# Ordering loads of v against transposed strips in the opening of a gated attention and mixer kernel

## The chip, the cores and the metric

The kernel runs on one core of one Trainium2 chip. The metric is the device time of one execution in microseconds (us), the median of several runs; less is better. A core has a matrix engine (TensorE, PE in the profile), three engines for elementwise work (VectorE, DVE; ScalarE, ACT; GpSimd, POOL) and a queue engine (SyncE, SP). Each works through its own list of instructions in order. Transfers run on 16 DMA engines, which are fed by two queues here: a software queue, whose transfers GpSimd issues, and a hardware queue, whose transfers SP issues.

## What is computed

```python
def _attn_ref(u, v, z):
    B, S, D = u.shape                                  # 8, 3136, 256; z has 64 columns
    scores = (1.0 / S) * np.matmul(z, z.transpose(0, 2, 1))
    attn = np.maximum(scores, 0.0) ** 2
    out = np.matmul(attn, v)
    return (u * out).astype(np.float32)

def _moe_ref(x, U, V, w_ch1, w_ch2):                   # x is the result of _attn_ref
    h = x.transpose(0, 2, 1) @ U @ V
    u = x + h.transpose(0, 2, 1)
    return (u + np.maximum(u @ w_ch1, 0.0) @ w_ch2).astype(np.float32)
```

The scores of a batch are a symmetric matrix of 3136 x 3136, and the same z stands on both sides. The change concerns the attention part alone.

## The kernel before

**Tiles.** The sequence of a batch is cut into NT = 25 blocks of 128 rows (the last, number NF = 24, has 64). The output block o is the sum over all blocks j of attn[j, o] times v[j]. As the score matrix is symmetric, only half of it is computed: tile `A[j]` holds the block row j against the NB = 13 blocks j to j + 12 (counted around the end). The other blocks that output o needs are transposes of blocks of `A[o]`. A DMA transpose on SP's queue writes them to a `strip`, 12 blocks of 128 x 128 in bf16 (`turn`, line 392). `block` (line 466) picks the tile: from `A[j]` when (o - j) mod 25 is at most 12, else from the strip of o.

**Order of outputs.** Outputs are taken from block 12 on (FIRST = 12): place i in the order is block 12 + i. LEAD = 16 is thus output 4 by place and LEAD + NG = 20 output 8 by place. Where the text below says output 16 to 24, blocks are meant. Two outputs form a pair that shares an accumulator; the first of a pair also takes the half row of block 24 for its partner (lines 551 to 554), so it ends with a read of the partner's strip.

**A score.** `score` (line 352) is a TensorE product of z with itself into PSUM, a ReLU on ScalarE (line 372) and a square on VectorE (line 374). A strip can go only when all of its `A` tile is squared.

**The opening.** `start_up` (line 768) does outputs 12 to 19 of batch 0 by hand, because nothing has been computed yet. For outputs 12 to 15 it makes the needed blocks directly. Meanwhile it scores `A[16]` to `A[19]` and turns each to a strip as soon as it is done (`turned`, line 437). Then outputs 16 to 19 are summed, first from `A`, then in `tail` (line 885) from the strips of 16, 17, 18 and 19 in this order; the steps of the list `rest` beside them make the blocks of `A[15]` to `A[8]` that output 20 needs. `turn(0, 20)` stands before `tail` in the program (line 884), and the strips of 21 and 22 are turned inside it. From place 8 on (output 20), the loop at line 957 runs `attend_steps` (line 526) for each output with the scores of later tiles spread between them.

**Loads of v.** The v of a batch comes in nine pieces (`V_PARTS`, line 311): eight of three blocks each, 192 KB in SBUF, cast to bf16 by the DMA, and the tail. All are issued by GpSimd, as are the loads of u (`load_u`, line 452) and of the weights. Batch 1's v isn't read until batch 0's outputs are done. Pieces 0, 1 and 2 are issued in the opening behind the weights (line 798). Pieces 3 and 4 stand behind a one-column GpSimd copy into the tile `mark`, which reads the strip of output 19 (line 869) and so holds GpSimd until that strip has landed. The tail piece and pieces 5 to 7 come later, out of the loop.

**Output 20.** For it alone the order of blocks is changed (line 530): five from `A` (20 down to 16), then the strip, then eight from `A` (15 down to 8).

**Queues.** SP's list holds only the transposes here, in program order: a strip that waits keeps the strips behind it from being issued. GpSimd's list holds its copies and loads, likewise in order.

Of the kernel before, what the change touches and what calls it, by code (L numbers as in the profile page):

```python
# [42 lines left out]
def kernel(  # L43
# [11 lines left out]
    nc = tc.nc  # L55

    B, S, D = u.shape
# [13 lines left out]
    NB = HALF + 1  # L71
    FIRST = HALF
    AHEAD = 4
    LEAD = FIRST + AHEAD
    NG = 4
# [20 lines left out]
    mark = persist.tile([P, 1], BF16, name="mark")  # L96
# [29 lines left out]
    v_both = [persist.tile([P, NT, D], BF16, name=f"v{k}") for k in range(2)]  # L126
# [5 lines left out]
    def turns(i):  # L132
        return (FIRST + i) % NT
# [168 lines left out]
    def load_v(b, part):  # L302
        t0, t1 = part
        v_bf = v_both[b % 2]
        if t0 < NF:
            pool_dma(out=v_bf[:, t0:t1, :], in_=rows(v[b])[:, t0:t1, :])  # L306
        else:
            for r in halves:
                pool_dma(out=v_bf[r, NF, :], in_=v[b, NF * P :, :])

    V_PARTS = [(t, t + 3) for t in range(0, NF, 3)] + [(NF, NT)]
# [36 lines left out]


    strips = {}  # L350

    def score(b, parts):

        ps = pair_psum()
        zT = zT_of(b)
        zT_flat = zT.rearrange("p t c -> p (t c)")
        at = (min(b, 1), 0)
        for k, (j, c, n, _) in enumerate(parts):
            mm(  # L359
                out=ps[:, k, :n],  # L360
                lhsT=zT[halves[k], j + at[k], :],
                rhs=zT_flat[halves[k], c + at[k] * P : c + at[k] * P + n],
                start=True,
                stop=True,
            )
        if parts[0][3] is parts[-1][3]:
            n = parts[0][2]
            todo = [(parts[0][3], ps[:, :, :n] if len(parts) == 2 else ps[:, 0, :n])]
        else:
            todo = [(part[3], ps[:, k, : part[2]]) for k, part in enumerate(parts)]  # L370
        for dst, src in todo:
            nc.scalar.activation(out=dst, in_=src, func=AF.Relu, scale=sc)  # L372
        for dst, _ in todo:
            nc.vector.tensor_tensor(out=dst, in0=dst, in1=dst, op=ALU.mult)  # L374
# [16 lines left out]

    def turn(b, o):
        strip = strip_pool.tile([P, HALF, P], BF16, name="strip")
        transpose(out=strip, in_=A[o][:, P:])
        strips[b, o] = strip

# [40 lines left out]
    def turned(b, j):  # L437
        steps = score_steps(b, j)
        s = steps.pop()
        return steps + [lambda: (s(), turn(b, j))]  # L440
# [5 lines left out]
    def pair_of(o):  # L446
        first = 0 if o < FIRST else FIRST
        stop = FIRST if o < FIRST else NT
        t0 = o - (o - first) % 2
        return t0, min(2, stop - t0)  # L450

    def load_u(b, o):
        t0, n = pair_of(o)
        u_sb = u_pool.tile([P, 2, D], FP32, name="u_sb")
        if o < NF:
            pool_dma(out=u_sb[:, :n, :], in_=rows(u[b])[:, t0 : t0 + n, :])  # L456
        else:
            for r in halves:
                pool_dma(out=u_sb[r, 0, :], in_=u[b, NF * P :, :])
        u_tiles[b, t0] = u_sb  # L460

    def open_pair(b, o):
        acc[pair_of(o)[0]] = sets[opened[0] % 2]
        opened[0] += 1

    def block(b, o, j):
        k = (o - j) % NT
        return A[j][:, k * P : (k + 1) * P] if k <= HALF else strips[b, o][:, NT - 1 - k, :]

    def half(b, o, j, h, w, start, stop, **kw):  # L470
        t0, _ = pair_of(o)
        mm(  # L472
            out=acc[t0][h][:, (o - t0) * D : (o - t0 + 1) * D],
            lhsT=w[halves[h]],
            rhs=v_both[b % 2][halves[h], j, :],
            start=start,
            stop=stop,
            **kw,
        )

    def close_pair(b, o):
        t0, n = pair_of(o)
        banks, u_sb = acc.pop(t0), u_tiles.pop((b, t0))
        w = n * D
        both = both_pool.tile([P, 512], FP32, name="both")
        nc.scalar.copy(out=both[:, :w], in_=banks[1][:, :w])  # L486
        nc.vector.tensor_tensor(  # L487
            out=both[:, :w], in0=banks[0][:, :w], in1=both[:, :w], op=ALU.add
        )
        if o == NF and b == 0:  # L490

            for bank in banks:
                for r in range(2):
                    q = both[halves[r], :w]
                    nc.vector.tensor_tensor(out=q, in0=bank[halves[1 - r], :w], in1=q, op=ALU.add)
        elif o == NF:
            for r in range(2):
                nc.scalar.copy(out=both[halves[r], w : 2 * w], in_=both[halves[1 - r], :w])
            nc.vector.tensor_tensor(
                out=both[:, :w], in0=both[:, :w], in1=both[:, w : 2 * w], op=ALU.add  # L500
            )
        nc.vector.tensor_tensor(  # L502
            out=x_at(b, t0, n),
            in0=split(both[:, :w]),
            in1=u_sb[:, :n, :].rearrange("p t (a c) -> p t a c", c=P),
            op=ALU.mult,
        )

    def quarter(b, j, n, h):

        c = n % 2
        mm(  # L512
            out=acc[NF][h][halves[c], :D],
            lhsT=block(b, NF, j)[halves[h], halves[c]],
            rhs=v_both[b % 2][halves[h], j, :],
            start=(n < 2),
            stop=(n == (NT - 2 if c else NT - 1 - 2 * h)),
        )

    def after(b, o):  # L520

        t0, n = pair_of(o)
        i = place(t0) + n
        return (b, turns(i)) if i < NT else (b + 1, turns(0))

    def attend_steps(b, o):
        t0, n = pair_of(o)
        last = t0 + n - 1
        js = [(o - k) % NT if k < NB else (o + k - HALF) % NT for k in range(NT)]
        if b == 0 and o == LEAD + NG:  # L530
            js = js[: NG + 1] + js[NB:] + js[NG + 1 : NB]
        js.remove(NF)

        def step(i):
            if i == 0 and o == t0:
                open_pair(b, o)
            if i == 16 and o == t0 and after(b, o)[0] < B:
                load_u(*after(b, o))
            if o == NF:
                if i < NT - 1 and i % 2:  # L540
                    for n in (i - 1, i):
                        for h in range(2):
                            quarter(b, js[n], n, h)
                elif i == NT - 1:
                    quarter(b, NF, i, 0)
            elif i < NT - 1:
                w = block(b, o, js[i])
                end = i == NT - 2
                half(b, o, js[i], 0, w, i == 0, end and o > t0)
                half(b, o, js[i], 1, w, i == 0 and o == t0, end)  # L550
            elif o == t0:
                half(b, o, NF, 0, block(b, o, NF), False, True)
                if o < last:
                    half(b, o + 1, NF, 1, block(b, o + 1, NF), True, False)
            if i == NT - 1 and o == last:
                close_pair(b, o)

        return [lambda i=i: step(i) for i in range(NT)]
# [209 lines left out]
    def start_up():  # L768
# [4 lines left out]
            out=eye,  # L773
            in_=eye,
# [20 lines left out]
            load_z(1, WHOLE)  # L795
        run(fetches)
        if B > 1:
            for part in V_PARTS[:3]:
                load_v(1, part)
        nxt = [s for j in range(LEAD, LEAD + NG) for s in turned(0, j)]  # L800
        rooms = [A[j % NT][:, : 2 * NG * P] for j in range(LEAD + NG, LEAD + 3 * NG)]
# [64 lines left out]
        ]  # L866
        run(_merge(nxt[2:], own))
        if B > 1:
            nc.gpsimd.tensor_copy(out=mark, in_=strips[0, LEAD + NG - 1][:, 0, :1])
            for part in V_PARTS[3:5]:  # L870
                load_v(1, part)
        rest = [
            lambda pair=pair: make_stored(pair, LEAD + NG)
# [3 lines left out]
        for i, pair in enumerate(pairs):  # L877
            if i + 2 < len(pairs):
                make_stored(pairs[i + 2], LEAD)
            else:  # L880
                more.pop(0)()
            use_stored(pair, outs)
            if i == len(pairs) - 1:
                turn(0, LEAD + NG)
        tail = []
        for o in outs:
            js = [(o + 1 + i) % NT for i in range(HALF)]
# [49 lines left out]

    fetches, second_w, puts, copies = weight_steps()
    panel = start_up()
    puts = dict(zip((17, 18, 19, 20, 16, 21, NT), puts + copies))  # L940
    late = []
# [6 lines left out]
    for b in range(B):  # L948
# [8 lines left out]
        for i in range(begin, NT):  # L957
            o = turns(i)
# [7 lines left out]
            if more:  # L966
# [14 lines left out]
                if b == 0 and i == 15:  # L981
                    mirror_z((0, FIRST))
                    extend_z(b + 1)
            main = attend_steps(b, o)
            if b and i in ahead:
                at = 17 if (i + (i > FIRST)) % 2 == 0 else 12 if i == 7 else 9 if i == 3 else 10
# [39 lines left out]
    b = B - 1  # L1026
# [46 lines left out]
```

## Time and profile before

| what | us |
|---|---|
| median of 3 runs (lowest to highest) | 995.57 (993.81 to 998.08) |
| profiled execution | 995.98 |
| span of the profiled execution | 994.3 |
| TensorE busy | 978.9 (98%) |
| TensorE weight loads busy | 815.5 (82%) |
| ScalarE busy | 615.5 (62%) |
| VectorE busy | 552.7 (56%) |
| GpSimd busy | 169.5 (17%) |
| hardware queue (transposes, last stores) | 371520 packets, 96.14 MB |
| software queue (loads, stores) | 28320 packets, 66.28 MB |

The span is what the profiler saw between the first and the last instruction; the execution's own time is 1.7 us longer. TensorE works at its full granted clock throughout (1.00). A row of a timeline gives start and duration in us, engine, line and operation, the tiles written and read, how many instructions were merged into it (x16), and in brackets the idle time of the engine before it with what ended it. "Landing" is the time from the issue of a transfer to its completion. Rows for stretches of time give, for TensorE, weight loads, VectorE, ScalarE and GpSimd in this order, the busy us and the number of instructions, then the granted clock, the mean busy share of the DMA engines and the GB/s that they moved.

Strips of the opening, from SP's queue:

| strip of output | issued at | landing after | landed |
|---|---|---|---|
| 16 | 20.22 | 11.0 | 31.2 |
| 17 | 26.60 | 8.4 | 35.0 |
| 18 | 30.51 | 7.0 | 37.5 |
| 19 | 33.05 | 5.6 | 38.7 |
| 20 | 37.07 | 3.8 | 40.9 |
| 21 | 38.95 | 8.7 | 47.7 |
| 22 | 40.92 | 13.7 | 54.6 |
| 23 | 47.16 | 9.9 | 57.1 |

Pieces of batch 1's v: issued at 17.94, 19.57 and about 20.1 (landed at 27.3, 28.9 and 30.0), and at 38.98 and about 39.5 (landed at 43.9 and 46.9).

### The profile page before, as it was taken

The page shows a single profiled execution, that of the slowest core. Times are in us where ns is not written, and L with a number is a line of the kernel's source. Part 1 is how long each engine was busy: PE and PEld are TensorE (multiplying, and loading weights), DVE is VectorE, ACT ScalarE, POOL GpSimd, SP SyncE. Part 2 cuts the span into 40 slices and gives each one's busy share as a digit, 9 for nine tenths or more (in the row PEclk, how much of TensorE's full clock was granted, in tenths as well). Part 3 has the DMA queues.
Part 4 walks back from the last instruction along what each step waited for, and adds up shares of the span by engine and source line. Part 5 has one row for each costly group of instructions (what it writes and reads, how often), then busy time and mean ns, then how long its engine had stood idle before and what let it go on. Part 6 is the DMA issues. An engine that isn't in the chain of part 4 may idle for free.

```text
span 994.3 us, 31019 instructions
## 1 busy us (share of the span) xinstructions
PE 978.9 (98%) x13632; PEld 815.5 (82%) x13672; DVE 552.7 (56%) x1025; ACT 615.5 (62%) x845; POOL 169.5 (17%) x317
## 2 busy tenths in 40 slices
PE   8899999999999999999999999999999999999998
PEld 6778878888788888788887888878888788788876
DVE  6779845567346574364653655546546466352342
ACT  8878764766647575475755757467574676643154
POOL 5111111112121111212112121121211201111000
PEclk9999999999999999999999999999999999999999
DMA  9999999899899998998989989889989796595443
GB/s 180 163 192 209 181 155 202 174 184 174 142 196 175 168 178 151 181 179 169 168 163 172 180 166 169 162 171 186 159 165 185 164 192 125 129 191 122 83 107 101
DMA packets 399976, 164.42 MB, mean 165 GB/s; under 512 B 375568, under 2 KB 384464, under 8 KB 399840
## 3 DMA queue, kind: packets, MB, share of 16 engines
q1 hardware_dynamic: 371520, 96.14, 61.5%
q0 software_dynamic: 28320, 66.28, 28.9%
q8 instruction: 107, 1.75, 0.8%
q14 instruction: 29, 0.24, 0.1%
HBM read 61.88 MB, written 25.69 MB: 88 GB/s over the span
## 4 chain that ended last, share of the span: by engine, by line
PE 95%; DMA 2%; DVE 1%; ACT 1%; issue 0%; POOL 0%; DVEq 0%; POOLq 0%
PE ps L472 51%; PE ps L701 17%; PE ps L654 17%; PE ps L359 7%; DMA strip<-A 1%; PE ps L622 1%; PE ps L512 1%; DMA v<-in_v_dram 1%; ACT A L372 1%; PE ps L567 1%; DVE A L374 0%; DMA out_dram<-o_sb 0%; DVE both L487 0%; ACT both L486 0%; DVE x_bf L502 0%
## 5 line engine op out<-in xcount | busy, mean ns | idle before, releaser
L372 ACT ACTIVATE A<-ps 128x832 bf16<-128x832 f32 (+9 forms) x481 | 358.4, 764 | 141.0 <-PE ps L359 135.6
L472 PE MATMUL ps<-v,A 64*128 64x256 bf16 x4988 | 341.2, 269 | 1.6 <-DVE A L374 1.1
L374 DVE TENSOR_TENSOR A<-A 128x832 bf16<-128x832 bf16 (+9 forms) x481 | 243.5, 523 | 135.4 <-ACT A L372 133.1
L472 PE MATMUL ps<-v,strip 64*128 64x256 bf16 x4420 | 310.3, 269 | 3.8 <-DMA strip<-A 3.0
L472 PEld LDWEIGHTS <-A 64*128 64x128 bf16 x4988 | 252.7, 94 | 40.0 <-issue 7.0
L672 ACT ACTIVATE relu_bf<-ps 128x1024 bf16<-128x1024 f32 (+2 forms) x208 | 188.3, 909 | 150.5 <-PE ps L654 144.7
L472 PEld LDWEIGHTS <-strip 64*128 64x128 bf16 x4420 | 227.6, 94 | 35.0 <-DMA strip<-A 4.6
L701 PE MATMUL ps<-w_bf,relu_bf 128*128 128x256 bf16 (+1 forms) x1600 | 201.4, 273 | 0.4
L654 PE MATMUL ps<-ut,w_bf 128*128 128x512 bf16 (+2 forms) x856 | 198.1, 353 | 1.7
L701 PEld LDWEIGHTS <-relu_bf 128*128 128x128 bf16 (+1 forms) x1600 | 153.0, 98 | 40.3 <-issue 4.9
L719 DVE TENSOR_TENSOR o_sb<-ps,x_bf 128x512 f32<-128x512 f32 (+2 forms) x81 | 54.8, 678 | 171.1 <-PE ps L701 166.1
L654 PEld LDWEIGHTS <-w_bf 128*128 128x128 bf16 x896 | 117.9, 144 | 37.4 <-issue 6.7
L359 PE MATMUL ps<-zT 64*128 64x416 bf16 (+8 forms) x812 | 134.8, 312 | 0.0
L456 POOL DMA_DIRECT2D u_sb<-in_u_dram x96 | 53.1, 554 | 444.4 <-DVE x_bf L502 426.3
L486 ACT COPY both<-ps 128x512 f32<-128x512 f32 (+1 forms) x104 | 59.0, 568 | 70.1 <-PE ps L472 64.0
L487 DVE TENSOR_TENSOR both<-ps,both 128x512 f32<-128x512 f32 (+1 forms) x104 | 69.3, 666 | 30.8 <-ACT both L486 30.2
L502 DVE TENSOR_TENSOR x_bf<-both,u_sb 128x512 bf16<-128x512 f32 (+1 forms) x104 | 69.8, 672 | 3.7
L636 DVE TENSOR_TENSOR x_bf<-ps,x_bf 128x512 bf16<-128x512 f32 (+1 forms) x112 | 65.5, 626 | 11.3 <-PE ps L622 11.2
L732 POOL DMA_DIRECT2D out_dram<-o_sb x66 | 36.1, 546 | 186.4 <-DVE o_sb L719 174.5
L359 PEld LDWEIGHTS <-zT 64*128 64x128 bf16 x812 | 46.3, 94 | 3.6
L719 DVE TENSOR_TENSOR both<-ps,x_bf 128x512 f32<-128x512 f32 (+1 forms) x24 | 15.0, 623 | 57.3 <-PE ps L701 57.3
L306 POOL DMA_DIRECT2D v<-in_v_dram x61 | 33.7, 556 | 3.9 <-issue 2.7
(65 smaller groups left out, 242.8 us busy)
## 6 DMA issues: line engine op xcount, KB each, us to landing
u_sb<-in_u_dram POOLq DMA_DIRECT2D x96, 256.0 KB, 4.2
out_dram<-o_sb POOLq DMA_DIRECT2D x66, 256.0 KB, 2.9
v<-in_v_dram POOLq DMA_DIRECT2D x57, 192.0 KB, 4.5
out_dram<-both POOLq DMA_DIRECT2D x18, 256.0 KB, 2.5
strip<-A SPq DMA_TRANSPOSE x194, 5.5
out_dram<-o_sb SPq DMA_DIRECT2D x11, 256.0 KB, 2.0
z_c<-in_z_dram POOLq DMA_DIRECT2D x7, 384.0 KB, 7.0
w_bf<-in_moe_w_ch_dram POOLq DMA_DIRECT2D x2, 512.0 KB, 7.6
```

The source lines that it names most:

```text
L359: mm(out=ps[:, k, :n], lhsT=zT[halves[k], j + at[k], :], rhs=zT_flat[halves[k], c + at[k] * P : c + at[k] * P + n], start=True, stop=True,)
L372: nc.scalar.activation(out=dst, in_=src, func=AF.Relu, scale=sc)
L374: nc.vector.tensor_tensor(out=dst, in0=dst, in1=dst, op=ALU.mult)
L472: mm(out=acc[t0][h][:, (o - t0) * D : (o - t0 + 1) * D], lhsT=w[halves[h]], rhs=v_both[b % 2][halves[h], j, :], start=start, stop=stop, **kw,)
L486: nc.scalar.copy(out=both[:, :w], in_=banks[1][:, :w])
L487: nc.vector.tensor_tensor(out=both[:, :w], in0=banks[0][:, :w], in1=both[:, :w], op=ALU.add)
L502: nc.vector.tensor_tensor(out=x_at(b, t0, n), in0=split(both[:, :w]), in1=u_sb[:, :n, :].rearrange("p t (a c) -> p t a c", c=P), op=ALU.mult,)
L636: nc.vector.tensor_tensor(out=q, in0=split(ps[h][:, : len(ks) * D]), in1=q, op=ALU.add)
L654: mm(out=ps[i][:, :w] if apart else ps[:, i, :w], lhsT=w1_at[:, db, hp + i, :], rhs=uT[c][:, db, len(chunks[c]) * P - w :], start=(db == 0 ...
L672: nc.scalar.activation(out=relus[c][:, hp : hp + 2, :w], in_=ps[:, :, :w], func=AF.Relu)
L701: mm(out=ps[r, k * D : (k + 1) * D], lhsT=relus[c][:, ht, q : q + (TAIL if two else P)], rhs=w2_bf[:, ht, :], start=(ht < 1 + two), stop=( ...
L719: nc.vector.tensor_tensor(out=o_sb[:p].rearrange("p t (a c) -> p t a c", c=P), in0=split(ps[:p, k0 * D : (k + 1) * D]), in1=x_at(b, t, nk) ...
```

## The change

Of batch 1's v, only pieces 0 and 1 are issued in the opening, and pieces 2, 3 and 4 behind the copy into `mark`, which now reads the strip of output 18, the third. Before the strips of outputs 16 and 20 are turned, GpSimd copies one column of a v piece into them (piece 1 for 16, piece 4 for 20). The transpose overwrites that column; but as the copy must wait for the piece to land, and the transpose for the copy, the strip isn't issued before the piece has landed. Output 20 takes nine blocks of `A` (20 down to 12), then its strip, then the four blocks 11 to 8.

```diff
     strips = {}
+    behind = {(0, LEAD): V_PARTS[1], (0, LEAD + NG): V_PARTS[4]} if B > 1 else {}
...
     def turn(b, o):
         strip = strip_pool.tile([P, HALF, P], BF16, name="strip")
+        if (b, o) in behind:
+            t = behind[b, o][1] - 1
+            nc.gpsimd.tensor_copy(out=strip[:, 0, :1], in_=v_both[1][:, t, :1])
         transpose(out=strip, in_=A[o][:, P:])
...
         if b == 0 and o == LEAD + NG:
-            js = js[: NG + 1] + js[NB:] + js[NG + 1 : NB]
+            js = js[: NG + 5] + js[NB:] + js[NG + 5 : NB]
...
-            for part in V_PARTS[:3]:
+            for part in V_PARTS[:2]:
                 load_v(1, part)
...
-            nc.gpsimd.tensor_copy(out=mark, in_=strips[0, LEAD + NG - 1][:, 0, :1])
-            for part in V_PARTS[3:5]:
+            nc.gpsimd.tensor_copy(out=mark, in_=strips[0, LEAD + NG - 2][:, 0, :1])
+            for part in V_PARTS[2:5]:
                 load_v(1, part)
```

In the changed kernel's list for GpSimd the new copies stand between the second v piece and the u loads of outputs 16 and 18, and between piece 4 and the u loads of outputs 20 and 22. Nothing else moves on GpSimd, and SP's list keeps its order.

## The prediction

> **What bounds the kernel now.** I read the page first. Of a span of 994.3 us TensorE is busy for 978.9, and the chain that ended last lies on it for 95%. A change that touches only transfers can therefore win no more than TensorE's idle time.
>
> ```profile
> span 994.3 us, 31019 instructions
> PE 978.9 (98%) x13632; PEld 815.5 (82%) x13672; DVE 552.7 (56%) x1025; ACT 615.5 (62%) x845; POOL 169.5 (17%) x317
> PE 95%; DMA 2%; DVE 1%; ACT 1%; issue 0%; POOL 0%; DVEq 0%; POOLq 0%
> ```
>
> Next, the waits of TensorE over the whole execution, longest first (columns: total us, times, longest):
>
> ```profile
> PE ps L472 <- DMA strip<-A: 3.0, 2, 1.8
> PE ps L359 <- ACT A L372: 2.4, 4, 1.0
> ...
> PE ps L472 <- DVE z_c L246: 0.8, 1, 0.8
> ```
>
> Then its timeline from 42 to 60 us, where these waits are:
>
> ```profile
> 42.63 0.74 PE L472 MATMUL ps<-v,A 64*128 64x256 bf16 x10
> 43.18 0.41 PE L472 MATMUL ps<-v,strip 64*128 64x256 bf16 x4
> ...
> 47.71 0.28 PE L472 MATMUL ps<-v,strip 64*128 64x256 bf16 x1 [1.80 <-DMA strip<-A]
> ...
> 54.64 0.72 PE L472 MATMUL ps<-v,strip 64*128 64x256 bf16 x10 [1.23 <-DMA strip<-A]
> ...
> 57.15 0.28 PE L472 MATMUL ps<-v,strip 64*128 64x256 bf16 x1 [0.81 <-DVE z_c L246]
> ```
>
> Output 20 begins at 42.63. The three waits are for the strips of outputs 21, 22 and 23. The last is put down to a DVE copy, but strip 23 lands at 47.16 + 9.9 = 57.06, just before the matmul, so I count it with the strips: 1.80 + 1.23 + 0.81 = **3.84 us**. Why they are late is in the times from issue to landing. Strip 20, issued at 37.07 with no other transfer in flight, lands after 3.8 us, at 40.9. Those issued at 38.95 (strip 21) and 40.92 (strip 22) need 8.7 and 13.7, and SP needs 6.05 us to issue the latter, against 1.44 for strip 20. Between them, from 38.98, GpSimd issues two v pieces (its timeline; columns: start, us, instruction, idle time before it):
>
> ```profile
> 19.57 1.06 POOL L306 DMA_DIRECT2D v<-in_v_dram  x2 [1.05 <-DMA z_c<-in_z_dram]
> ...
> 38.75 0.22 POOL L869 COPY mark<-strip 128x1 bf16<-128x1 bf16 x1 [9.62 <-DMA strip<-A]
> 38.98 1.08 POOL L306 DMA_DIRECT2D v<-in_v_dram  x2
> 42.20 0.55 POOL L456 DMA_DIRECT2D u_sb<-in_u_dram  x1 [2.14 <-DVE x_bf L502]
> 45.95 0.54 POOL L456 DMA_DIRECT2D u_sb<-in_u_dram  x1 [3.20 <-DVE x_bf L502]
> ```
>
> In stretches of the same trace (last column: GB/s moved), strips and other loads together run well at one time and badly at others:
>
> ```profile
> 30.00:34.00 4.00, 3.82 (x67) 3.39 (x69) 3.51 (x11) 3.98 (x10) 0.00 (x0) 1.00 1.31 292
> 41.00:46.00 5.00, 4.77 (x77) 4.05 (x73) 4.89 (x13) 4.67 (x10) 0.60 (x2) 1.00 1.28 135
> 48.00:53.00 5.00, 4.89 (x83) 4.33 (x80) 2.60 (x5) 3.90 (x7) 0.00 (x0) 1.00 1.09 109
> 54.00:55.00 1.00, 0.36 (x8) 0.33 (x10) 1.00 (x3) 0.36 (x1) 0.90 (x2) 1.00 1.30 298
> ```
>
> From 41 to 46 the mix is strips with v pieces, from 48 to 53 strips with two u tiles and the two small tail pieces of v. From 30 to 34 it is strips with two u tiles, at 292 GB/s.
>
> **The change, part by part.** TensorE, ScalarE and VectorE keep every instruction; in the built program only the order of output 20's blocks differs on TensorE. DMA bytes are the same. Added are two one-column GpSimd copies; the nearest row, `mark`, took 0.22 us each.
>
> *The opening.* One 192 KB piece fewer is issued at 20 us. The three pieces there landed at 27.3, 28.9 and 30.0. The software queue moved 0.42 MB after 24.0; without the third piece's 0.196 MB, 0.22 MB are left, at the 0.19 MB/us of 15 to 24 some 1.2 us, and about 1 us to land. I take the second piece at 26.3, between 25.2 (no tail) and 28.9 (as now). Strip 16, ready at 20.2 and now issued then, goes at about 26.6. Strips 17 and 18 stand behind it on SP (their squares end at 24.6 and 27.0) and strip 19 too (29.3). Without v beside them I give each 1.7 us of the engines (0.39 MB at the 0.25 MB/us of 57 to 58 is 1.6): landings 30.4, 32.1, 33.8, 35.5, against 31.2, 35.0, 37.5, 38.7 now. TensorE first reads them at 35.6, 37.1, 38.7 and 40.3, so the hold is covered by 5 us. Cover gone: at the late end (28.9) strip 16 goes at 29.2, and by the same steps lands at 33, still 2.6 ahead. On GpSimd the u loads at 26.75 and 28.58 stand behind the new copy; they feed products at 41.2 and 45.0, so a delay of 2 us costs nothing.
>
> *The three pieces.* They go when strip 18 lands, 33.8 + 0.3 = 34.1, and take 3 x 0.54 us to issue: the last at 35.2. 0.59 MB at 0.17 to 0.19 MB/us is 3.1 to 3.5 us; with the 4.5 us that a piece takes in the middle of all 57 the last lands at 39.7 to 40.3. I take **40.0**. The ends are 38.5 and 46.3 (strip 18 landing at 37.5 as now, last issue at 38.9, and the 7.4 us that the later piece of 39 us takes now).
>
> *The second hold.* Strip 20, ready at 37.04, goes at 40.0 + 0.3 = 40.3, lands after its unmixed 3.8 us at 44.1, and I add 0.5 for the u load of 42.2 that now runs beside it: **44.6**. Queued on SP behind it are strips 21 (ready 38.9) and 22 (40.6): at 1.7 us each they land at about 46.3 and 48.0. Strip 23 (ready 46.8) has SP free. On GpSimd the u load of 42.2 stands behind the copy that ends at 40.3, so it isn't moved.
>
> *The order of output 20.* Its strip is read after nine blocks of A and no longer after five: 42.63 + 18 x 0.055 + one score pair of 0.18 = 43.8, against 43.2. Blocks 15 to 12 must be squared by then; VectorE's row of eight squares begins at 41.83 and the fourth ends near 43.2, when TensorE wants the first at 43.2 and the fourth at 43.6. So no wait is added, by a margin of 0.3 us. Were it gone, it would cost tenths.
>
> *Sum.* Removed: 3.84. Added: strip 20 lands at 44.6 and is wanted at 43.8, 0.8. Strip 21 is wanted at 45.9 + 0.8 = 46.7 and lands at 46.3; 22 is wanted near 51.6 + 0.8 and lands at 48.0; 23, issued near 47, near 51 to 52 with u beside it, is wanted at about 54. I take off 0.3 because scores (ScalarE 4.19 of 5 us from 50 to 55) set the pace once or twice more when TensorE is earlier. Net gain 3.84 - 0.8 - 0.3 = **2.7 us**. Behind 60 us TensorE is without gaps to 125 us, and its work with ScalarE's and VectorE's moves forward as a whole. Profiled execution: 995.98 (span 994.3) becomes 993.3 (span 991.6). The runs' median, 995.57, lies 0.4 under the profiled one: 992.9.
>
> The Trainium skill, "DMA: Bandwidth & Descriptors", section "Issuing engines are not separate DMA queues", says that DMAs of all issuers run on the same 16 DMA engines and interleave; by that alone keeping two kinds apart saves no byte, and holding a ready strip only delays it. The rows of 109 to 135 against 292 GB/s speak for a loss in mixing, which the rule doesn't give; what order alone would make is the third rival.
>
> **The rivals.**
> *No new wait:* v lands at 38.5 to 39.2, strip 20 by 43.5. All 3.84 us go and nothing comes: 995.57 - 3.84 = 991.7. For it: pieces alone have little in front of them after 34. Against: it needs every term at its early end.
> *u slows them as well:* the 109 GB/s stretch holds hardly any v, so strips 22 and 23 may stay late. Then 1.23 + 0.81 stay, 1.80 goes, 0.8 comes: 994.6. Against: 30 to 34 us, u and strips at 292.
> *Only the order counts:* the engines lose nothing in mixing, and 0.196 MB more lie ahead of strips 21 to 23, at 0.19 MB/us 1.0 us more: 996.6. Against: the stretches above.
> *The second hold takes over, slower:* output 20 waits for a chain of one strip landing, three pieces, a copy, then a whole strip. At the late end above (v at 46.3) strip 20 goes at 46.6 and lands at 50.4 alone, or at 51.5 with u beside it: a wait of 6.6 to 7.7, with 21 to 23 behind it hidden; less 3.84, +2.8 to +3.9; with the 8.7 us that strip 21 needed amid loads, up to +7.7. Middle +5: 1000.6. It decides from a landing of strip 20 after 43.8 + 3.84 = 47.6, that is v after 43.5. For it: the landings of today. Against: v now starts when one strip, not two, is left ahead.
> That the holds do nothing can be excluded: the built program has the waits.
>
> **Numbers.** Forecast 0.38, no new wait 0.27, u 0.11, order only 0.06, second hold 0.18. I call 0.5%, 5 us, what a measurement of this kernel can tell from no change (the three runs lie 4.3 apart). Below 990.6 fall about 0.13 of the forecast and 0.4 of "no new wait" by the runs' scatter: 0.05 + 0.11 = 0.16. Above 1000.6 falls 0.6 of the second hold, 0.11, and 0.01 of the rest: 0.12. Within: 0.72. Range 990.0 to 999.0 (a tenth on each side left out); the forecast's own is 991 to 995.
>
> **What would show it.** Strip 16 issued at 26 to 27 instead of 20.2; strip 18 landed by 34; the three pieces issued at 34 to 35 and landed by 40; strip 20 issued at 40.3 and landed in 4 to 5 us; the waits of 1.80, 1.23 and 0.81 gone, one of some 0.8 us near 44 ahead of output 20's strip. A strip 18 after 36, v pieces after 42, or issues of strips that still take 4 to 6 us would make it wrong.

## The result: slower, and the profile after

The changed kernel took 1001.35 us (median of 7 runs, 997.66 to 1003.30) against 995.57 before (7 runs, 993.81 to 998.13). The ratio is 1.005, with a 95% interval of 1.0031 to 1.0069: slower by some 5 us, or half a percent, where 2.7 us less were forecast. Executions over 1.5% longer than the fastest of the same kernel are left out of all figures below.

The profiled execution was the shortest of the seven: 997.66 us, with a span 1.7 us over that of before. Its lines are four further down (L476 is L472 of before, L397 the new copy). The page, then TensorE's waits:

```profile
span 996.0 us, 31024 instructions
PE 979.7 (98%) x13632; PEld 816.2 (82%) x13672; DVE 552.6 (55%) x1025; ACT 615.1 (62%) x845; POOL 170.4 (17%) x319
```

```profile
PE ps L476 <- DMA strip<-A: 5.1, 1, 5.1
PE ps L360 <- ACT A L373: 2.4, 4, 1.0
```

The three waits of before (1.80, 1.23, 0.81) are gone, as forecast. In their place is one, of 5.07 us; the waits for ScalarE, the next largest, stand at 2.4 as before. TensorE's timeline shows it in the middle of output 20, at the first read of its strip:

```profile
42.83 0.41 PE L476 MATMUL ps<-v,A 64*128 64x256 bf16 x4
48.31 2.29 PE L476 MATMUL ps<-v,strip 64*128 64x256 bf16 x20 [5.07 <-DMA strip<-A]
```

The second row has more in it. Twenty such products take 1.1 to 1.3 us elsewhere, and 2.29 here. The stretches of 1 us from 48 on (the last three columns are the granted clock, the DMA share and GB/s) show why: the clock is at one half from 48.4 to 51.8.

```profile
48.00:49.00 1.00, 0.69 (x8) 0.64 (x10) 0.00 (x0) 0.00 (x0) 0.00 (x0) 0.69 1.02 278
49.00:50.00 1.00, 1.00 (x14) 0.85 (x12) 0.00 (x0) 0.00 (x0) 0.00 (x0) 0.50 1.27 204
50.00:51.00 1.00, 1.00 (x12) 0.75 (x10) 0.00 (x0) 0.02 (x1) 0.00 (x0) 0.50 1.31 262
51.00:52.00 1.00, 1.00 (x14) 0.88 (x12) 0.12 (x1) 0.85 (x1) 0.00 (x0) 0.60 1.28 268
52.00:53.00 1.00, 1.00 (x22) 0.94 (x19) 0.47 (x1) 0.17 (x1) 0.00 (x0) 1.00 0.11 21
```

What set the end of the wait is in the chain of work that ended last (start, us, what):

```profile
31.43 5.61 DMA strip<-A
37.04 0.05 issue
37.09 0.19 POOL mark L873
37.28 0.05 issue
37.33 1.61 POOL v L306 x3
38.93 3.87 issue
42.80 0.04 POOLq L460
42.84 0.66 POOL strip L397
43.50 0.02 issue
43.52 4.66 DMA strip<-A
48.17 0.14 issue
48.31 2.29 PE ps L476 x20
```

This is the chain of the prediction's fourth rival, link by link: strip 18 lands (37.0), GpSimd reads it, three pieces are issued, they land (the "issue" of 3.87 us), the copy into strip 20, a whole strip, and only then TensorE. Strip 18 was forecast for 33.8.

The account of the span: +5.07 for the new wait, -3.84 for the old ones, +1.7 for 3.4 us of work at half clock, and -0.75 because TensorE was ahead before the wait (its clock rose to 1.00 at 4.0 us and not at 5.5, and the first v piece landed after 5.7 us instead of 6.9; such things differ from run to run). That is +2.2, against 1.7 measured. A landmark in both traces places the half microsecond: ScalarE's copies at the ends of two pairs of outputs (line 486, L490 after) begin at 43.51 and 51.70 before, at 42.76 and 55.83 after. Between them 4.88 us more passed, 5.07 - 1.80 for waits and 1.6 for the clock; behind them the missing waits for strips 22 and 23 gave back 2.4 and not 2.04. The six other executions were longer still, and each of the seven had a mean clock between 0.994 and 0.998. The first question was therefore what a longer one looks like.

### The profile page after: what moved, and what is told of

The parts are those of the page before. It is cut to its first block, busy times and chain, and to the rows that moved or that the text cites. A ratio compares the mean times of both kernels' runs of the same rounds, so it can differ in the third digit from the quotient of the medians.

```text
span 996.0 us, 31024 instructions
## 1 busy us (share of the span) xinstructions
PE 979.7 (98%) x13632; PEld 816.2 (82%) x13672; DVE 552.6 (55%) x1025; ACT 615.1 (62%) x845; POOL 170.4 (17%) x319
## 4 chain that ended last, share of the span: by engine, by line
PE 95%; ACT 2%; DMA 1%; issue 1%; DVE 1%; POOL 0%; DVEq 0%; POOLq 0%
PE ps L476 50%; PE ps L705 17%; PE ps L658 17%; PE ps L360 7%; ACT A L373 2%; PE ps L626 1%; PE ps L516 1%; DMA strip<-A 1%; PE ps L571 1%; DMA out_dram<-o_sb 0%; PE ps L269 0%; ACT both L490 0%; POOL v L306 0%; DVE o_sb L723 0%; DVE A L375 0%
## 5 line engine op out<-in xcount | busy, mean ns | idle before, releaser
L476 PE MATMUL ps<-v,A 64*128 64x256 bf16 x4988 | 341.3, 269 | 1.3 <-DVE A L375 1.1
L476 PE MATMUL ps<-v,strip 64*128 64x256 bf16 x4420 | 310.9, 270 | 5.1 <-DMA strip<-A 5.1
L476 PEld LDWEIGHTS <-A 64*128 64x128 bf16 x4988 | 252.7, 94 | 40.0 <-issue 6.4
L476 PEld LDWEIGHTS <-strip 64*128 64x128 bf16 x4420 | 228.0, 94 | 35.8 <-issue 5.3
L705 PEld LDWEIGHTS <-relu_bf 128*128 128x128 bf16 (+1 forms) x1600 | 152.9, 98 | 40.3 <-issue 4.9
L658 PEld LDWEIGHTS <-w_bf 128*128 128x128 bf16 x896 | 117.9, 144 | 37.5 <-issue 6.7
L490 ACT COPY both<-ps 128x512 f32<-128x512 f32 (+1 forms) x104 | 59.1, 568 | 70.0 <-PE ps L476 64.0
L360 PEld LDWEIGHTS <-zT 64*128 64x128 bf16 x812 | 46.3, 94 | 3.6
```

Of the source, the lines that this page charges most:

```text
L360: mm(out=ps[:, k, :n], lhsT=zT[halves[k], j + at[k], :], rhs=zT_flat[halves[k], c + at[k] * P : c + at[k] * P + n], start=True, stop=True,)
L476: mm(out=acc[t0][h][:, (o - t0) * D : (o - t0 + 1) * D], lhsT=w[halves[h]], rhs=v_both[b % 2][halves[h], j, :], start=start, stop=stop, **kw,)
L658: mm(out=ps[i][:, :w] if apart else ps[:, i, :w], lhsT=w1_at[:, db, hp + i, :], rhs=uT[c][:, db, len(chunks[c]) * P - w :], start=(db == 0 ...
L705: mm(out=ps[r, k * D : (k + 1) * D], lhsT=relus[c][:, ht, q : q + (TAIL if two else P)], rhs=w2_bf[:, ht, :], start=(ht < 1 + two), stop=( ...
```

## The experiments

Kernels of one group ran on one chip beside the kernel before. The column "full clock" counts executions whose mean granted clock was 0.999 or 1.000.

| kernel | median us | ratio to before (95%) | full clock |
|---|---|---|---|
| the change, first comparison | 1001.35 | 1.005 (1.0031 to 1.0069) | 0 of 7 |
| again | 1000.19 | 1.0037 (1.0015 to 1.0059) | 0 of 10 |
| no_hold_20 | 1002.06 | 1.0058 (1.0036 to 1.0081) | 0 of 10 |
| no_hold_16 | 995.0 | 1.0001 (0.9975 to 1.0027) | 6 of 10 |
| no_hold_16_2 | 996.48 | 1.0009 (0.998 to 1.0039) | 5 of 12 |
| no_holds | 992.28 | 0.999 (0.9955 to 1.0025) | 7 of 9 |
| no_holds_2 | 996.51 | 1.0013 (0.9984 to 1.0043) | 6 of 12 |
| u_after_20 | 997.59 | 1.0015 (0.9992 to 1.0039) | 0 of 10 |
| u_after_17 | 999.08 | 1.0034 (1.0007 to 1.0061) | 0 of 9 |
| u_after_both | 999.3 | 1.0016 (0.9988 to 1.0045) | 1 of 10 |
| late_pieces | 993.88 | 0.998 (0.9953 to 1.0007) | 8 of 10 |
| late_pieces_2 | 994.85 | 1.0002 (0.9982 to 1.0023) | 7 of 12 |
| two_then_late | 993.87 | 0.9997 (0.9962 to 1.0032) | 8 of 11 |
| hold_16_late | 993.19 | 0.9983 (0.9953 to 1.0012) | 7 of 10 |
| wait_short | 1002.07 | 1.0076 (1.005 to 1.0103) | 0 of 9 |
| wait_long | 1008.07 | 1.0125 (1.0067 to 1.0183) | 0 of 4 |

The kernel before stood at full clock in 17 of 30, 14 of 24, 18 of 33 and 12 of 29 executions of the groups behind the first comparison.

**again: a second trace of the change.** No edit.

> The changed kernel once more, for a second trace. In its first trace TensorE waits 5.07 us for the strip of output 20 (43.24 to 48.31) and then runs at a granted clock of 0.50 to about 51.6, though that execution (997.66) was the shortest of seven; the others had mean clocks of 0.997 to 0.994. Theory: the wait ends in a stretch at half clock whose length differs from run to run, so an execution of 1000 us or more shows the same wait of 4 to 7 us and a longer stretch below 1.0 behind it (a mean clock of 0.995 is 10 us at one half). Rival: the longer executions have longer waits or a second wait elsewhere, and the clock has no part in it: then the clock behind the wait is low for no more than 4 us again.

```profile
51.03 2.32 PE L476 MATMUL ps<-v,strip 64*128 64x256 bf16 x20 [7.81 <-DMA strip<-A]
```

The wait is 7.81 us (1000.69 us, span 999.0). Up to the hold it is nearly as in the first trace: strip 18 lands at 37.0, the last piece at 43.2 (42.8 there), strip 20 is issued at 43.5. But it takes 7.4 us to land, where it took 4.7. The clock falls at 48.3 again, 5.1 us after the last product, and is whole at 55.2, so 4.1 us of work run at half: 2.1 us more. 7.81 - 3.84 + 2.1 - 0.75 = 5.3, measured 4.7 (by the same landmark the clock took 1.9, and the missing waits gave back 2.4 here too). The theory (a longer stretch at half: 6.8 us against 3.4) and the rival (a longer wait) are each right in part; most of the added stretch lies inside the wait, and the wait is the larger part.

**no_hold_20 and no_hold_16: one hold each.** `behind` keeps one of its entries.

```diff
-    behind = {(0, LEAD): V_PARTS[1], (0, LEAD + NG): V_PARTS[4]} if B > 1 else {}
+    behind = {(0, LEAD): V_PARTS[1]} if B > 1 else {}              # no_hold_20
+    behind = {(0, LEAD + NG): V_PARTS[4]} if B > 1 else {}         # no_hold_16
```

> The change without the hold of output 20's strip; the first hold, the three pieces behind strip 18 and the new order stay. Theory (the second hold makes the loss): no wait above 3 us on TensorE near 43 to 50, granted clock 1.000, and strips 20 to 22 beside the pieces, so 2 to 4 us of waits for strips as before: 993 to 997 us. Rival (the loss is in the moved pieces or the first hold): 999 us or more and a mean clock under 0.998.

> The change without the hold of output 16's strip; the second hold stays. Theory: strip 16 is issued at 20 again, strip 18 lands near 36 to 37.5, so the wait for strip 20 stays at 4 to 6 us and the clock falls behind it: 998 to 1002 us. Rival (the first hold is what delays strip 18): strip 18 lands by 34, the wait falls to 2 us or less, clock 1.000, 993 to 995 us.

Both fell out against my theory. Without the second hold nothing is won: strip 20 is issued at 37.3, but strip 21, at 38.9, meets the pieces of 37.9 to 39.5, lands after 13.8 us, and TensorE waits for it instead:

```profile
44.26 1.26 PE L476 MATMUL ps<-v,strip 64*128 64x256 bf16 x20 [0.40 <-DMA strip<-A]
52.70 0.39 PE L476 MATMUL ps<-v,strip 64*128 64x256 bf16 x1 [6.35 <-DMA strip<-A]
```

Without the first hold the loss is gone. In this trace strip 18 landed at 33.7, the pieces at 39.8 and strip 20 was issued at 40.05, the path of the prediction (33.8, 40.0, 40.3), and the clock stayed whole. But strip 20 took 5.5 us to land beside the u load of 41.5, where 4.3 were forecast, so the wait was 2.44 and not 0.8, and strip 23 brought another of 0.88:

```profile
45.72 1.27 PE L476 MATMUL ps<-v,strip 64*128 64x256 bf16 x20 [2.44 <-DMA strip<-A]
```

The span was 993.4 us, 0.9 under that of before and not 2.7. So the loss needs the first hold, and the second neither makes nor mends it.

**no_holds, no_holds_2, no_hold_16_2: is it strip 18?** `behind = {}`; and no_hold_16 once more.

> The change with neither hold; the moved pieces and the new order of output 20 stay. Theory (the first hold loses 3 us of transposing, and three pieces that run into strips 20 to 22 cost another wait when they go as late as 37 to 39): without the first hold strip 18 lands near 34, the pieces go at 34 to 36 and land by 40, strip 20 is issued at 37 beside their second half, and the waits for strips 20 to 23 add up to 1 to 3 us with a clock of 1.000: 993 to 995.5 us. Rival (without the second hold strips and pieces collide whatever the time): one wait over 4 us and a clock of 0.998 or less, 998 us or more.

> no_holds once more, for a trace of an ordinary execution (the first was a disturbed one) and a closer interval. Theory (it is the first hold that makes strip 18 late): strip 18 lands at 33 to 35, the pieces go before 36, no wait over 3 us for strips 20 to 23, clock 1.000 in at least half the executions, 992 to 994 us and not slower than the kernel before. Rival (strip 18 lands at 37 to 39 without the hold too, as in the disturbed trace, and the first hold is innocent): one wait over 4 us in the trace, 997 us or more.

> no_hold_16 once more. Theory: strip 18 lands by 35, pieces by 41, the wait for strip 20 is 1.5 to 3.5 us, clock 1.000 in at least half the executions, 993.5 to 996 us. Rival: strip 18 at 37 or later, the wait over 4 us, 998 us or more.

The trace of no_holds is of an execution of 1012.05 us, so its rows aren't used here; the kernel's other executions were the shortest of the study when at full clock (a median of 992.0 of seven). The two later traces are of executions below full clock, and show that the rival has a point: strip 18 can be late without the hold too. In no_holds_2 it landed at 36.5, and strip 21 after 12.1 us; in no_hold_16_2 at 38.6, the pieces at 45.4, strip 20 at 51.7:

```profile
50.29 0.39 PE L476 MATMUL ps<-v,strip 64*128 64x256 bf16 x1 [4.29 <-DMA strip<-A]
```

```profile
51.85 2.32 PE L476 MATMUL ps<-v,strip 64*128 64x256 bf16 x20 [7.67 <-DMA strip<-A]
```

Taken together: without the first hold strip 18 landed anywhere from 33.7 to 38.6, and 24 of 43 executions kept the full clock. With it, strip 18 landed at 37.0, 37.0, 37.7 and 37.0 in four traces (the change twice, no_hold_20, u_after_20), and of 37 executions none did (of u_after_17 and u_after_both, which have the hold and move u as well, 1 of 19). The first hold doesn't always make strip 18 later; it takes the early cases away. That is narrower than my expectation, and the counts, not one landing, carry it.

**u_after_20, u_after_17, u_after_both: the u loads.** GpSimd reads a strip before it issues the u loads, so that these start when that strip has landed.

```diff
                 if o == outs[1]:
+                    nc.gpsimd.tensor_copy(out=mark, in_=strips[0, LEAD + NG][:, 0, :1])   # u_after_20
                     load_u(0, LEAD + NG)
...
         outs = [LEAD + i for i in range(NG)]
+        nc.gpsimd.tensor_copy(out=mark, in_=strips[0, LEAD + 1][:, 0, :1])                # u_after_17
         for o in outs[::2]:
             open_pair(0, o)
             load_u(0, o)
```

> The change with one more copy: GpSimd reads strip 20 before it issues the u loads of outputs 20 and 22, so that these start when the strip has landed. Theory (the spread of the changed kernel between 997 and 1004 comes from the u load issued in the same moment as strip 20, which made it land after 4.7 us in one trace and 7.4 in the other): strip 20 lands in 3.7 to 4.3 us, the wait is 4 to 5 us, executions lie closer together, 996 to 999 us. Rival (the strip is slow for another reason): it lands after 5 to 8 us again, 999 us or more.

> The change, with the u loads of outputs 16 and 18 held back until strip 17 has landed (a GpSimd copy of its first column). Theory (the step of the prediction that failed, 1.7 us for each of strips 16 to 18, failed because two u loads ran beside them): strip 16 lands near 30.3, 17 near 32, 18 by 34.5 to 35; the pieces land near 41, the wait for strip 20 falls from 5 to 8 us to 3 to 5: 996 to 999 us. Rival (strips held and then sent in a row are slow without u too): strip 18 near 37 again and the time as of the change, 1000 us.

> The change with both moves of u: those of outputs 16 and 18 behind strip 17 and those of 20 and 22 behind strip 20. This clears the way that the prediction took for granted. Theory: strip 18 by 35, pieces by 41, strip 20 issued at 41.3 and landed at 45.1, a wait of 1.5 to 2.5 us against 43.2, too short for the clock to fall: 992.5 to 994.5 us, clock 1.000. Rival (the waits shift to strips 21 to 23, beside which u now runs, or u comes late for the products of outputs 16 to 21): 996 us or more.

With u behind strip 20, that strip lands 3.8 us after its issue, as in the kernel before, the wait is 4.19 us, and executions lie between 996.6 and 999.5 where the change spreads from 997.5 to 1004.4:

```profile
47.70 2.31 PE L476 MATMUL ps<-v,strip 64*128 64x256 bf16 x20 [4.19 <-DMA strip<-A]
```

So the loads that GpSimd issues right behind the hold, the first of u in the same moment as strip 20, cost that strip 0.9 to 3.6 us, and the narrower range says that they make most of the spread. The clock falls all the same (at 45.8, whole at 52.6).

For strips 16 to 18 the u loads explain half. From the issue of 16 to the landing of 18 took 10.6 us in the change, 8.7 in u_after_17 and 9.2 in u_after_both; I had forecast 7.2. In neither did the time follow: v piece 1 landed later here (27 to 28 against 26), and the u loads now ran beside the three pieces, which in u_after_both landed only at 45.0. The waits were 9.98 and 5.64 us, both still for strip 20. The rival of u_after_17 is right (strip 18 at 37.3, the time as of the change); that of u_after_both has the time right, but not the way: the wait didn't shift to strips 21 to 23, the pieces were late. A collision moved was a collision kept.

**late_pieces, two_then_late, hold_16_late: the pieces out of the opening.** From the kernel before, without the copy into `mark`; pieces 3 and 4 (or 2 to 4) go singly at places 12 and 14 (12, 14, 16). hold_16_late adds the first hold to two_then_late.

```diff
-        if B > 1:
-            nc.gpsimd.tensor_copy(out=mark, in_=strips[0, LEAD + NG - 1][:, 0, :1])
-            for part in V_PARTS[3:5]:
-                load_v(1, part)
...
-        v_at = dict(zip((17, 20, 22, 10), V_PARTS[5:]))
+        v_at = dict(zip((12, 14, 17, 20, 22, 10), V_PARTS[3:]))        # late_pieces
+        v_at = dict(zip((12, 14, 16, 18, 20, 22, 10), V_PARTS[2:]))    # two_then_late, with V_PARTS[:2] in the opening
```

> The kernel before, with pieces 3 and 4 of v moved out of the opening to places 12 and 14 of the loop, and no copy into mark; no hold at all. Theory (the pieces of 39 us make strips 21 to 23 late): the waits of 1.80, 1.23 and 0.81 us shrink to 1 us or less in all, nothing comes in their place, 991.5 to 993.5 us. Rival (the u loads slow the strips as well): 1.5 to 2.5 us of waits for strips 22 and 23 stay, 993.5 to 995 us.

> late_pieces once more on the chip of the two above, to see which is the shortest: waits for strips under 1 us in all, clock 1.000 in three executions of four, 992.5 to 994.5 us, below the kernel before with an interval that ends under 1.000. If v pieces in the loop cost as much later as they save here, it is level with the kernel before.

> The kernel before with pieces 0 and 1 of v in the opening and pieces 2 to 7 one at a time in the loop (places 12, 14, 16, 18, 20, 22); no copy into mark, no hold, the old order of output 20. Theory (v pieces near the strips of outputs 20 to 23 are the whole of the loss, and a wait long enough to halve the clock is what makes some executions of the kernel before slow): no wait for a strip over 0.5 us, mean clock 0.999 or 1.000 in nearly all executions, 991.5 to 993.5 us and a narrower spread than the kernel before. Rival (the opening's strips or u loads collide as well): 994 us or more, some executions under 0.999.

> two_then_late with the first hold of the change: strip 16 behind piece 1. Theory (the first hold has no price of its own, only through the pieces chained to strip 18): strips 16 to 19 land 0 to 3 us later than without it but before TensorE reads them, no wait over 0.5 us, the time of two_then_late within 1 us. Rival (the first hold alone delays TensorE): a wait of 1 us or more near 35 to 41 us, 994 us or more.

In all four traces the waits for strips 20 to 23 are gone, and nothing above 1.3 us (for a strip of a later output, near 68 us) comes instead. The two largest groups of TensorE's waits in late_pieces_2, over the whole span (total, times, longest), are the same waits for ScalarE and 1.5 us for strips:

```profile
PE ps L359 <- ACT A L372: 2.4, 4, 1.0
PE ps L472 <- DMA strip<-A: 1.5, 2, 1.3
```

Spans are 991.9, 991.8, 990.7 and 991.2 us, against 994.3 to 995.7 in three traces of the kernel before. So v pieces do make strips 21 to 23 late, the 3.84 us can be had, and the rival by u is out: u and strips alone are no burden there. The first hold, alone, costs TensorE nothing: strips 16 to 19 land at 33.5, 36.2, 37.5 and 38.9 and no product waits for them. It does move strip 18: two_then_late, the same kernel without it, landed that strip at 34.2, in one trace each. Its price comes only through the pieces chained to strip 18. But the medians don't show a gain clear of noise: the intervals reach 1.0007, 1.0023, 1.0032 and 1.0012, since part of the executions fell below full clock here too, against what I had expected of late_pieces_2 and two_then_late, and for those I have no trace. late_pieces is no slower than either kernel and its trace is free of the loss; shorter than before isn't shown.

**wait_short, wait_long: what a wait costs by itself.** late_pieces, with strip 20 kept back by work on GpSimd, and no transfer added. The loads that GpSimd issues behind this work start later too.

```diff
         strip = strip_pool.tile([P, HALF, P], BF16, name="strip")
+        if (b, o) == (0, LEAD + NG):
+            nc.gpsimd.tensor_copy(out=mark, in_=A[o][:, NB * P - 1 :])
+            for _ in range(5):      # wait_long: 9
+                nc.gpsimd.memset(strip, 0.0)
```

> The kernel of late_pieces with a wait made by hand: GpSimd reads the last column of A[20] and then clears strip 20 five times (some 1.0 us each, by the memsets of 0.14 and 0.20 us for 32 and 128 columns) before it is turned. No transfer is added. Strip 20 lands near 46 instead of 40.7, and TensorE waits 2.5 to 3.5 us. Theory (a wait costs its own length until it lasts 4 to 5 us, then the clock falls to one half for 3 to 5 us of work): granted clock 1.000, 2 to 3.5 us over late_pieces, 996 to 997.5 us. Rival (any wait of some us lowers the clock): clock 0.998 or less, 998 us or more.

> As wait_short with nine clearings: TensorE waits 6.5 to 9 us. Theory: the granted clock drops to 0.50 some 4.5 to 5.5 us after TensorE's last matmul and stays there until 3 to 5 us after it goes on; the time is late_pieces plus the wait plus 1.5 to 2.5 us: 1002 to 1005 us, mean clock 0.995 to 0.997. Rival (the clock has no price of its own): late_pieces plus the wait alone, and matmuls at full rate behind it.

A clearing took 1.43 us and not 1.0, so the waits were 5.86 and 12.57 us: the short one was too long to test its own theory. For the long one the theory holds in kind: the clock fell 2.9 us after the last product, sooner than I had written, and stayed at one half until 59.5, 4 us into the work:

```profile
55.46 0.61 PE L476 MATMUL ps<-v,strip 64*128 64x256 bf16 x4 [12.57 <-DMA strip<-A]
```

```profile
58.00:59.00 1.00, 1.00 (x12) 0.69 (x10) 0.00 (x0) 0.00 (x0) 0.00 (x0) 0.50 0.01 2
59.00:60.00 1.00, 1.00 (x16) 0.75 (x14) 0.00 (x0) 0.64 (x1) 0.00 (x0) 0.77 0.00 0
```

Spans are 8.6 and 13.3 us over late_pieces (991.9). The same landmark gives the price of the clock. From one of ScalarE's copies to the next (43.42 to 49.59 in late_pieces, 43.18 to 57.67 and 43.02 to 63.87 here) 8.32 and 14.68 us more passed. Taking the waits of 5.86 and 12.57 off leaves 2.5 and 2.1 us, for 4.7 and 4.0 us of work at one half. So the long one's rival (the clock has no price of its own) is wrong. Up to the end other waits change too: wait_short has two more, of 1.18 and 1.25 near 70 and 77, the long one 0.59 near 82.

**before_a, before_b: the kernel before.** Unchanged, one execution each.

> The kernel before, unchanged, for another trace: of its executions beside the other kernels some half had a mean clock of 0.998 or less. Theory (a wait for a strip of more than 2.3 us can halve the clock here too): if this execution is at 0.998 or less, it has one wait for strip 21, 22 or 23 of 3 to 6 us near 45 to 57 and a stretch at 0.50 behind it, and is 2 to 5 us longer than 994; if it is at 1.000, the longest wait is under 3 us. Rival (the clock falls without a wait, anywhere): the stretch below 1.0 stands away from a wait for a strip.

> The same once more: mean clock 0.998 or less only with a wait for a strip of over 2.3 us and the stretch at 0.50 behind it.

```profile
49.07 0.28 PE L472 MATMUL ps<-v,strip 64*128 64x256 bf16 x1 [3.41 <-DMA strip<-A]
```

```profile
50.00:53.00 3.00, 3.00 (x56) 2.76 (x54) 1.36 (x3) 2.53 (x4) 0.00 (x0) 1.00 1.07 102
```

```profile
48.91 0.39 PE L472 MATMUL ps<-v,strip 64*128 64x256 bf16 x1 [3.10 <-DMA strip<-A]
```

```profile
50.00:53.00 3.00, 3.00 (x30) 2.15 (x28) 0.59 (x1) 1.06 (x2) 0.00 (x0) 0.50 1.13 141
```

The first two fences are before_a, the last two before_b. Strip 21 was later in both than in the profile that the prediction was made from (wait 1.80). In before_a 3.41 us passed at full clock, where I had expected no wait over 3: 56 products in the 3 us. In before_b 3.10 us halved it, from about 47.8 to 54.6: 30 products in the same 3 us. So the kernel before stands at the edge: its wait for strip 21, 1.8 to 3.4 us in three traces, tips the clock in some executions; the last section shows what decides. The changed kernel's, 5.07 and 7.81 in its two traces, tips it, and none of its 17 executions stood at full clock.

## Why the prediction was wrong, point by point

*Removed, 3.84 us:* right in kind. None of the waits for strips 21 to 23 is left in the traces of the change, and late_pieces shows that they come from the v pieces. In the change they are hidden behind the new wait rather than cured: strips 21 and 22 landed at 51.5 and 52.7, forecast 46.3 and 48.0. Its size belonged to one execution; 4.8 and 3.1 us stood there in two others (before_a and before_b).

*The opening and the first hold:* piece 1 landed at 26.1 (forecast 26.3) and strip 16 was issued at 26.4 (26.6). TensorE didn't wait for strips 16 to 19, as forecast.

*Strip 18 at 33.8 is the step that failed:* "Without v beside them I give each 1.7 us of the engines". It landed at 37.0. From the issue of strip 16 that is 10.6 us where 7.2 were forecast; u_after_17 and u_after_both put 1.5 to 1.9 us of the 3.4 on the two u loads. The rest stayed without them: the first strip took 4.0 to 4.5 us and not 3.8, and the next two came 2.1 and 2.6 us apart on average and not 1.7. I had priced them by one microsecond of the trace (57 to 58). The prediction had 37.5 as the late end, "as now", and treated it as unlikely; before_a and before_b, the same kernel as that "now", landed the strip at 35.2 and 35.4.

*The pieces:* 5.7 and 6.2 us from strip 18's landing to theirs in the two traces, forecast 6.2. The copy behind them took 0.67 and 0.23 us. Right.

*Strip 20 behind its hold:* "I add 0.5 for the u load of 42.2 that now runs beside it". The term was 0.9 in one trace and 3.6 in the other, against the 3.8 us of u_after_20, which holds u and the tail pieces back. In no_hold_16, where all ahead of it went as forecast, it was 1.8. The prediction had said that this load "isn't moved". It was: at a hold that ends at 43, it starts together with the strip.

*Wanted at:* 43.2 and not 43.8, because TensorE began earlier in these executions; the new order of output 20 did what was forecast and added no wait for squares.

*The wait by its terms:* 5.07 us are 4.3 more than the 0.8 forecast: 3.2 from strip 18, -0.5 from the pieces, 0.5 from the copy (0.67 us) and the issue behind it, 0.4 from strip 20, 0.6 because TensorE wanted it earlier, 0.1 between landing and product. In the second trace, 7.0 more, strip 18 gives 3.2 and strip 20 gives 3.1.

*A term was missing:* what a wait does to the clock. 3.4 to 4.1 us of work at one half cost 1.6 and 1.9 us in the two traces of the change. The Trainium skill states it, in "TensorE: Matmul & The Clock Gate", section "HAM oscillation — how this bites in real kernels": no gaps of TensorE above some 3.4 us. The prediction weighed another page and passed this one by. The traces agree in kind; the length that counts here is in the last section.

*Two readings of the views, and the range:* strip 20 did not go "with no other transfer in flight", since strip 19 landed at 38.7 and a v piece was issued at 38.98, both before its landing at 40.9; and the stretch from 41 to 46 held the u load of 42.20 beside strips and v. The range was to leave "a tenth on each side" out, but the prediction's own 0.12 above 1000.6 puts more than a tenth above 999.

The fourth rival is what happened, by its chain and its point of decision for strip 20 (landed after 47.6: 48.2 and 50.9). By its condition for v it would not have come: v landed at 42.8 and 43.2, not after 43.5, and the rest came from strip 20 itself. That its price (1000.6) is so near the 1000.19 and 1001.35 measured is in part luck, since it has no term for the clock. It was given 0.18, against 0.65 for the two cases that need strip 18 before 34. The views already spoke for it: the only landing of strip 18 on hand was 37.5, and each link of the chain was priced at its unmixed best. A chain of transfers in series is not a sum of best cases.

What is shown, by executions of kernels with one part undone: the first hold together with three pieces issued at strip 18's landing makes the loss, with or without the second hold. What is argued only: that the constancy of strip 18's landing near 37, and no other effect of that hold, is the link.

## What to carry to other kernels

A transfer that is held back so that it doesn't collide loses the time in which it could have run alone, and whatever is chained behind it starts later; price the whole chain by the landings that the trace shows among other traffic, and follow what a released engine issues in the same instant. A wait of TensorE can have a second price beyond its length, 1.6 to 2.5 us in the traces here. By the rows of the last section a wait of up to 1.8 us alone has none and one of 4 us (twice 2.0) or more always has it, which is an estimate from this kernel alone. So one wait of 5 us can cost what three of 1 to 2 us don't. When a kernel's executions scatter, look at the mean clock of each before comparing medians: a change can move the share of executions that tip.

## What the runs showed of the hardware that was not expected

The granted clock has two values here, 1.00 and 0.50. It fell after TensorE had been idle for 2.0 us (before_b), 2.3 (u_after_20), 2.4 (u_after_17), 2.5 (no_holds_2), 2.9 (wait_long), 3.7 (u_after_both), 3.8 (wait_short), 4.3 (no_hold_16_2), 4.5 (no_hold_20) and 5.1 (the change, twice), and didn't fall in waits of 2.44 (no_hold_16) and 3.41 (before_a). It is no fixed delay. The changes lie on a grid instead. The stretches at one half lasted 3.41 us (48.38 to 51.79, the change), 6.83 (again, before_b and most others), 10.24 (u_after_17) or 13.65 (wait_long): one, two, three or four times 3.41. The full clock ahead of them lasted 40.96 or 44.37 us, twelve or thirteen times 3.41, counted from the moment at which it first rose (3.9 to 7.3 us into the span, another in each execution).

Cut into steps of 3.41 us from that moment, all traces follow one rule. A step at full clock in which TensorE was idle for at most 1.85 us in all left the clock alone, and the clock fell at the end of each step with 1.98 us or more. Idle time is a step's length less TensorE's busy time, the first two numbers behind the start and end. The first two rows are of before_a, the third of before_b:

```profile
43.81:47.22 3.41, 1.85 (x33) 1.51 (x27) 2.61 (x5) 1.77 (x3) 1.52 (x3) 1.00 1.25 123
47.22:50.64 3.42, 1.57 (x28) 1.42 (x30) 0.00 (x0) 0.53 (x1) 0.09 (x1) 1.00 1.35 139
44.38:47.80 3.42, 1.43 (x25) 1.09 (x19) 2.24 (x4) 1.36 (x2) 1.61 (x3) 1.00 1.32 119
```

The border of two steps cut the wait of 3.41 us in before_a into two parts with 1.56 and 1.85 us of idle time; of the 3.10 us in before_b, 1.99 fell into one step. So which executions of the kernel before tip is a matter of where its wait lies on the grid. The same page of the Trainium skill, section "What's actually happening", gives 3.4 us for such a window and says that it runs free. It names one idle window as what throttles; in before_b a window idle for 1.99 of its 3.41 us was enough.

A DMA transpose of one strip landed 3.8 us after its issue with no load beside it (strip 20 in u_after_20 and u_after_both), and up to 14.7 us beside loads of the software queue (strip 22 in before_a), with the same bytes. In the worst mixed stretches both queues together moved 102 GB/s (before_a, 50 to 53) to 135 (before, 41 to 46), in the best 292 (before, 30 to 34). Which of the two it will be I could not tell from the traces.
